# Loading seven of twelve strided row ends tensor by tensor, and keeping pieces of the channel mix out of the last six modes

## The chip, the cores and the metric

One core of a Trainium2 chip runs one program. The metric is the device time of one execution in microseconds (us). A profiled span is some 1.8 us shorter than the time of the same run, because it leaves out what lies before the first and after the last instruction. Spans are used for where time goes, times for how much. In the views, PE is the engine for matmuls (PEld its weight loads), DVE, ACT and POOL are the vector, scalar and GpSimd engines; `L547` is line 547 of the kernel.

## The reference

Local and strided causal attention (8 batches, 8 heads, 576 positions, head size 64) feeds a spectral layer: 64 complex 512 x 512 weight matrices, one for each mode, then an inverse transform and a channel mix.

```python
def _attn_ref(q, k, v):
    ...
    mask_local = (rel >= 0) & (rel < stride)                       # heads 0 to 3
    mask_strided = (rel >= 0) & (pos[None, :] % stride == pos[:, None] % stride)
    ...                                                            # softmax, times v

def _moe_ref(x, w_r, w_i, w_ch):
    X = np.fft.rfft(x, axis=1)
    Xr, Xi = np.real(X[:, :64]), np.imag(X[:, :64])
    Yr = einsum('bmd,mde->bme', Xr, w_r) - einsum('bmd,mde->bme', Xi, w_i)
    Yi = einsum('bmd,mde->bme', Xr, w_i) + einsum('bmd,mde->bme', Xi, w_r)
    Y[:, :64] = Yr + 1j * Yi
    u = x + np.fft.irfft(Y, n=S, axis=1)
    return u + np.maximum(u @ w_ch, 0.0)
```

## The kernel before

All large loads go out from GpSimd in one order. The strided heads of q, k and v come two batches at a time: a body of 64 partitions, and the **rest** of 8 partitions, each for two batches ("two tensors" below). The other q, k and v loads are the local heads, 128 partitions with rows of 1152 elements. The weights are tiles of two modes.

```python
def load_str(b, nb):
    for vi in (2, 0, 1):                         # v, q, k
        n = 3 * (b % 4) + SLOT[vi]
        two = ring[:, n : n + 4 : 3, :]          # two batches
        src = SRC[vi][b - b % 2 : b - b % 2 + 2, 4:8].rearrange(
            "b h (c r) d -> (h c) b (r d)", r=32)
        if nb == 2:
            nc.gpsimd.dma_start(two[0:64], src[0:64])
        else:
            nc.gpsimd.dma_start(ring[0:64, n, :], src[0:64, b % 2])
        if b % 2 == 0:
            nc.gpsimd.dma_start(two[64:72], src[64:72])      # the rest
```

With b = 0, 2, 4, 6 and three tensors there are twelve rests. In the second half of the kernel (the second 256 input channels), each mode is 16 small matmuls on its weight tile; between modes the PE does 76 pieces of other work (turns and pieces of the channel mix), and then the first matmuls of the tail.

```python
LATE = 10
first = len(work) - 2 * LATE
for m in range(NM - 3):                          # NM = 64
    mode(1, m)
    if m < NM - 3 - LATE:
        upto = -(-first * (m + 1) // (NM - 3 - LATE))
    else:
        upto = first + 2 * (m - (NM - 4 - LATE))
    for w in work[n:upto]:
        w()
    n = upto
    if m >= 16 and m % 16 in (4, 8):
        spec(m // 16 - 1, 0 if m % 16 == 4 else 1)   # inverse transform of 16 modes
# ...
for i in range(3):
    if i < 2:
        v_early(i)
    u_early(i)
warm = psum("v")
# ...
for m in range(NM - 3, NM):
    mode(1, m)
again(2)                                         # matmuls that only keep the clock up
spec_last(0)                                     # last 16 modes; then the tail
```

The softmax here doesn't subtract the row's maximum and nothing guards it: scores larger than these inputs give would overflow.

## Time and profile before

| | before |
|---|---|
| time, median of 4 runs | 436.77 us (436.56 to 436.91) |
| profiled span | 434.8 us |
| written by DMA | 92.16 MB |
| last weights land | 393.77 us |
| last-spectrum matmuls (`spec_last`) start | 398.02 us |
| from there to the end of the span | 36.8 us |

Read the table from the bottom: the end of the kernel has a fixed length, so what counts is when `spec_last` starts, and that needs the last weights and a free PE. The prediction below shows the page's slices and the chain of this kernel.

### The profile page before, as it was taken

The page shows a single profiled execution, that of the slowest core. Times are in us where ns is not written, and L with a number is a line of the kernel's source. Part 1 is how long each engine was busy: PE and PEld are TensorE (multiplying, and loading weights), DVE is VectorE, ACT ScalarE, POOL GpSimd, SP SyncE. Part 2 cuts the span into 40 slices and gives each one's busy share as a digit, 9 for nine tenths or more (in the row PEclk, how much of TensorE's full clock was granted, in tenths as well). Part 3 has the DMA queues.
Part 4 walks back from the last instruction along what each step waited for, and adds up shares of the span by engine and source line. Part 5 has one row for each costly group of instructions (what it writes and reads, how often), then busy time and mean ns, then how long its engine had stood idle before and what let it go on. Part 6 is the DMA issues. An engine that isn't in the chain of part 4 may idle for free.

```text
span 434.8 us, 12063 instructions
## 1 busy us (share of the span) xinstructions
PE 334.7 (77%) x5289; PEld 241.1 (55%) x5289; DVE 215.0 (49%) x466; ACT 188.0 (43%) x353; POOL 129.3 (30%) x208
## 2 busy tenths in 40 slices
PE   1987988789876879787865567679596769888994
PEld 1865776667765666665753345445454445554442
DVE  2788788744452242442511034244335443764895
ACT  1587678635542433534440302113313312443883
POOL 6423332323232222222222222222222222200893
PEclk9999899869895585988885559585769687999999
DMA  8999999999999999999999999999999999980787
GB/s 174 210 212 213 214 212 213 211 210 212 214 214 212 214 213 214 214 213 214 214 213 213 213 213 214 214 214 213 213 213 214 213 213 215 213 176 13 268 316 287
DMA packets 28995, 92.16 MB, mean 212 GB/s; under 512 B 4048, under 2 KB 5072, under 8 KB 28944
## 3 DMA queue, kind: packets, MB, share of 16 engines
q0 software_dynamic: 24704, 81.28, 94.2%
q1 hardware_dynamic: 3440, 9.46, 5.8%
q10 hardware_dynamic: 800, 0.67, 0.6%
q8 instruction: 41, 0.67, 0.6%
q14 instruction: 10, 0.08, 0.0%
HBM read 163.22 MB, written 9.44 MB: 397 GB/s over the span
## 4 chain that ended last, share of the span: by engine, by line
DMA 73%; PE 19%; DVE 2%; issue 2%; ACT 1%; POOL 1%; DVEq 0%; POOLq 0%
DMA wt<-in_moe_w_i_dram 51%; DMA ring<-in_v_dram 7%; DMA ring<-in_k_dram 6%; DMA wt<-in_moe_w_r_dram 4%; DMA ring<-in_q_dram 4%; PE sc L645 3%; PE y L547 3%; PE v L688 2%; PE u L688 2%; PE v L890 2%; PE y L514 1%; PE tp L653 1%; DVE yy L678 1%; PE u L911 1%; DVE xT L597 1%
## 5 line engine op out<-in xcount | busy, mean ns | idle before, releaser
L547 PE MATMUL y<-X,wt 128*128 128x16 f16 (+1 forms) x2048 | 82.4, 192 | 63.5 <-DMA wt<-in_moe_w_i_dram 60.9
L547 PEld LDWEIGHTS <-wt 128*128 128x128 f16 (+1 forms) x2048 | 72.6, 103 | 75.6 <-issue 72.3
L196 POOL DMA_DIRECT2D wt<-in_moe_w_r_dram x62 | 36.5, 589 | 142.2 <-PE y L547 63.1
L196 POOL DMA_DIRECT2D wt<-in_moe_w_i_dram x60 | 35.4, 590 | 70.6 <-DMA wt<-in_moe_w_i_dram 57.9
L654 ACT ACTIVATE v<-sc 128x512 f16<-128x512 f32 x32 | 18.9, 597 | 86.1 <-PE sc L645 86.0
L645 PE MATMUL sc<-w_cp,xT 128*128 128x512 f16 (+1 forms) x160 | 51.3, 450 | 0.4 <-DVE xT L617 0.4
L471 ACT ACTIVATE PL<-sc 128x480 f16<-128x480 f32 (+1 forms) x48 | 27.6, 579 | 47.4 <-PE sc L457 46.9
L655 DVE COPY xo<-tp 128x512 f16<-128x512 f16 x32 | 22.1, 692 | 45.5 <-PE tp L653 45.5
L250 DVE TENSOR_TENSOR xb<-av,rec 90x256 f16<-90x256 f32 (+2 forms) x80 | 36.0, 450 | 2.8
L249 DVE RECIPROCAL rec<-av 90x4 f32<-90x4 f32 (+2 forms) x80 | 14.7, 183 | 42.1 <-PE av L486 31.3
L402 DVE COPY qT<-tp 128x576 f16<-128x576 f16 x16 | 12.0, 758 | 42.8 <-PE tp L395 39.4
L260 ACT ACTIVATE v<-tp 128x640 f16<-128x640 f16 (+1 forms) x24 | 19.4, 808 | 21.2 <-PE tp L429 17.8
L395 PE MATMUL tp<-cI_s,ring 64*64 64x64 f16 x864 | 26.4, 210 | 2.2 <-issue 1.4
L360 ACT ACTIVATE PL<-sc 90x360 f16<-90x360 f32 (+1 forms) x48 | 22.7, 490 | 5.6 <-PE sc L353 4.9
L922 DVE TENSOR_TENSOR osb<-u,rl 128x512 f32<-128x512 f32 x36 | 23.6, 688 | 2.6 <-PE u L688 1.3
L395 PEld LDWEIGHTS <-ring 64*64 64x64 f16 x864 | 20.6, 122 | 7.4 <-issue 4.4
L905 POOL TENSOR_TENSOR rl<-rl,xo 128x512 f32<-128x512 f32 x16 | 18.3, 1156 | 20.5 <-ACT rl L903 20.2
L441 PE MATMUL sc<-cMl_s,cI_s 128*128 128x480 f16 (+1 forms) x48 | 22.4, 467 | 1.6 <-ACT X L260 1.6
L260 ACT ACTIVATE kz<-tp 64x360 f16<-64x360 f16 (+1 forms) x32 | 19.0, 595 | 10.2 <-PE tp L395 8.6
L457 PE MATMUL sc<-qT,kz 128*128 128x160 f16 (+1 forms) x160 | 22.6, 267 | 0.2 <-issue 0.2
L645 PEld LDWEIGHTS <-xT 128*128 128x128 f16 (+1 forms) x160 | 14.5, 109 | 14.6 <-issue 5.7
L285 PE MATMUL tp<-cI_s,ring 72*128 72x72 f16 x256 | 15.1, 206 | 9.5 <-DMA ring<-in_v_dram 8.0
(103 smaller groups left out, 647.8 us busy)
## 6 DMA issues: line engine op xcount, KB each, us to landing
wt<-in_moe_w_r_dram POOLq DMA_DIRECT2D x62, 512.0 KB, 18.9
wt<-in_moe_w_i_dram POOLq DMA_DIRECT2D x60, 512.0 KB, 19.4
out_dram<-osb SPq DMA_DIRECT2D x14, 512.0 KB, 2.7
ring<-in_v_dram POOLq DMA_DIRECT2D x8, 288.0 KB, 13.4
ring<-in_q_dram POOLq DMA_DIRECT2D x8, 288.0 KB, 13.6
ring<-in_k_dram POOLq DMA_DIRECT2D x8, 288.0 KB, 13.2
ring<-in_v_dram POOLq DMA_DIRECT2D x3, 512.0 KB, 15.5
ring<-in_q_dram POOLq DMA_DIRECT2D x3, 512.0 KB, 14.9
```

The costliest lines, as they stand in the source:

```text
L196: nc.gpsimd.dma_start(dst, rows)
L250: nc.vector.tensor_tensor(out=dst, in0=val.rearrange("p h (q c) -> p h c q", c=4), in1=rec[0:n, 0:pieces] .to_broadcast((n, pieces, 64)) . ...
L260: nc.scalar.activation(out=out, in_=in_, func=ACTF.Copy)
L360: nc.scalar.activation(out=PS[0:n, ds(POFF[t], 4 * n)], in_=scp[0:n, 0 : 4 * n], func=ACTF.Exp, scale=SCALE,)
L395: nc.tensor.transpose(tp[ds(64 * hp, 64), ds(64 * i, 64)], qn[ds(64 * hp, 64), ds(64 * (9 * g + i), 64)], idn[ds(64 * hp, 64), ds(64 * hp, ...
L441: nc.tensor.matmul(scp[:, 0 : n * times].rearrange("p (h x) -> p h x", h=times), idn, mask_rows("cMl", n, times), start=True, stop=False,)
L457: nc.tensor.matmul(scp[:, ds(col, n)], kzs[par][:, hp, ds(s0, 128)], qTs[par][:, ds(s0, n)], start=False, stop=(i == len(todo) - 1),)
L471: nc.scalar.activation(out=dst, in_=src, func=ACTF.Exp, scale=SCALE)
L547: nc.tensor.matmul(yv[:, mi, e, :], wt[pr, XC[c], ds(128 * e, 128)], Xh[half][pr, c, :, :, m], start=(c == 0), stop=(c == 3),)
L645: nc.tensor.matmul(vp[pr, :], xT[:, ch, cols], w_chs["cp"][:, ch, :], start=(ch == 0), stop=(ch == 3),)
L655: nc.vector.tensor_copy(out=xo[pr].rearrange("p (h q c) -> p h q c", h=2, c=4), in_=tp[pr, 0:512].rearrange("p (h c q) -> p h q c", h=2, c=4),
L922: nc.vector.tensor_tensor(out=osb[:, t % 2, :], in0=up, in1=rls[b, t][:, t % 2, :], op=AluOp.add)
```

## The change

Its intent: spread the small rests better over the DMA engines, and leave nothing but weights and PE work for them in the last six modes. The pieces must then be done three modes sooner; `LATE` goes from 10 to 12, and the first matmuls of the tail move in between the last modes, with a few more of the matmuls that keep the clock up.

```diff
--- before.py
+++ after.py
@@ -227,8 +227,14 @@
                 nc.gpsimd.dma_start(two[0:64], src[0:64])
             else:
                 nc.gpsimd.dma_start(ring[0:64, n, :], src[0:64, b % 2])
-            if b % 2 == 0:
+
+
+
+            if b % 2 == 0 and 3 * (b // 2) + SLOT[vi] < 5:
                 nc.gpsimd.dma_start(two[64:72], src[64:72])
+            elif b % 2 == 0:
+                for j in range(2):
+                    nc.gpsimd.dma_start(two[64:72, j], src[64:72, j])
 
     def load_loc(*bs):
         for b in bs:
@@ -836,14 +842,15 @@
 
     n = 0
 
-    LATE = 10
+    LATE = 12
+    END = NM - 6
     first = len(work) - 2 * LATE
-    for m in range(NM - 3):
+    for m in range(END):
         mode(1, m)
-        if m < NM - 3 - LATE:
-            upto = -(-first * (m + 1) // (NM - 3 - LATE))
+        if m < END - LATE:
+            upto = -(-first * (m + 1) // (END - LATE))
         else:
-            upto = first + 2 * (m - (NM - 4 - LATE))
+            upto = first + 2 * (m + 1 - (END - LATE))
         for w in work[n:upto]:
             w()
         n = upto
@@ -940,20 +947,22 @@
                 osb,
             )
 
-    for i in range(3):
-        if i < 2:
-            v_early(i)
-        u_early(i)
-    warm = psum("v")
 
 
     def again(n):
         for i in range(n):
             nc.tensor.matmul(warm, idn, v0s[0][:, 2, :], start=True, stop=True)
 
-    for m in range(NM - 3, NM):
+    early = [lambda i=i: v_early(i) for i in range(2)]
+    early += [lambda i=i: u_early(i) for i in range(3)]
+    warm = psum("v")
+    for m in range(END, NM):
         mode(1, m)
-    again(2)
+        if m < END + 2:
+            for w in early[3 * (m - END) : 3 * (m - END) + 3]:
+                w()
+        else:
+            again(3 if m < NM - 1 else 2)
     spec_last(0)
     again(3)
     v_early(2, warm)
```

Line numbers shift with it: `spec_last`'s matmuls are L882 before and L889 after, a mode is L547 and L553.

## The prediction

> **What bounds the kernel now.** I read three views in this order: the slices, the chain of the end in order of time, and the GpSimd timeline beside it. The slices first (PEclk is the granted TensorE clock in tenths, a slice is 434.8 / 40 = 10.87 us):
>
> ```profile
> PEclk9999899869895585988885559585769687999999
> DMA  8999999999999999999999999999999999980787
> GB/s 174 210 212 213 214 212 213 211 210 212 214 214 212 214 213 214 214 213 214 214 213 213 213 213 214 214 214 213 213 213 214 213 213 215 213 176 13 268 316 287
> ```
>
> For 35 slices the DMA engines are full at 213 GB/s written (the loads convert f32 to f16, so twice that is read). These are the weights, and no rearrangement of compute changes that part. The time is then set by two things: when the last weight lands, and how long after it the kernel ends. The last loads, in the GpSimd timeline (start us, us, engine, line, operation, in brackets the idle time before and its releaser):
>
> ```profile
> 381.48 0.52 POOL L199 DMA_DIRECT2D wt<-in_moe_w_i_dram  x1 [1.94 <-DMA wt<-in_moe_w_r_dram]
> 384.00 0.52 POOL L199 DMA_DIRECT2D wt<-in_moe_w_i_dram  x1 [2.00 <-DMA wt<-in_moe_w_i_dram]
> DMA to landing us min/median/max: 9.8/10.7/11.7
> ```
>
> (The last line is the answer for the weight tile in the window from 380.) Issued at 384.00 and 9.8 us under way, the last weights land at 393.8. The chain then shows (start us, us, what):
>
> ```profile
> 390.47 0.48 PE y L547 x16
> 390.95 0.86 PE sc L645 x4
> ...
> 393.28 0.70 DVE xoh L655
> 394.03 0.39 PE v L890
> ...
> 394.85 0.43 PE u L911 x2
> 395.28 0.49 PE y L547 x16
> 395.86 0.57 DVE YT L575
> 396.47 1.12 PE y L547 x32
> 397.59 0.43 PE v L952 x2
> 398.02 0.99 PE y L882 x4
> ```
>
> Each L547 group of 16 is one mode. Mode 60 runs at 390.47, then come its two pieces of the channel mix (L645 and L653), the DVE copy that frees their PSUM banks, the five early matmuls, mode 61 at 395.28, and modes 62 and 63 only from 396.47. Nothing in this stretch waits for a DMA: all weights are there from 393.8, and mode 63 starts at about 397.0. So in the last 10 us the **PE queue is the bound**, not the weight stream. From the last-spectrum matmuls (L882, 398.02) to the end at 434.8 are 36.8 us that the change does not touch.
>
> **Why the last weights come as late as 393.8.** The trace keeps sixteen completion records for each load, one for each DMA engine. For the last load eight are between 387.37 and 389.36 and the other eight between 392.82 and 393.77: half of the engines run 5.1 us behind (means of the two halves). This gap is 0.7 us at 14 us, about 0.95 at 60 us, 2.0 at 140, 3.5 at 229, 4.2 at 301 and 5.1 at the end, so it grows steadily long after the rests are loaded. What grows with it are the 41 packets of the instruction queue, 16 KB and about 0.94 us each: their times repeat in a pattern of eight, and 34 fall between 60 and 390 us, so 34 x 0.94 / 8 = 4.0 us on each of eight engines. That is the growth. Following the packets by their spacing (305 ns from one 4 KB packet to the next on an engine), the engines that carry instruction packets are those that get the data of the even rests (v of batch pair 4, k of 4, q of 6); I trust this grouping only fairly.
>
> **What the Trainium skill says.** (1) "DMA: Bandwidth & Descriptors", section "Why a DMA increments its semaphore by 16 and not by 1": the number of engines is the largest k up to 16 that divides the slowest dimensions, so eight partitions give k = 8, on consecutive engines from a round-robin cursor; but some direct copies from GpSimd get k = 16 with partitions/16 rounded up per engine, which for eight partitions would be always the first eight engines. The trace agrees with the first for the rests of two tensors: between 37 and 64 us an engine shows two packets for one rest and none for the next, in turn. For a rest of one tensor no instruction of this kernel tells which of the two holds. (2) "TensorE: Matmul & The Clock Gate", Part 1: the clock is either full or half, decided over windows of 3.4 us of activity. The trace agrees: the clock records are 1.0 or 0.5 and change in multiples of 3.41 us; half from 354.4 to 364.7, then full until 432.9. (3) Same page, "Back-to-back issue gap": 216 ns for 512 columns warm; here four take 0.86 us, 215 ns each.
>
> **Part 1, the rests.** Seven of twelve loads of 8 partitions x 2 tensors (16 packets) become two of 8 packets each. No byte is added; 7 more GpSimd issues of 0.52 to 0.58 us lie in a queue that spends most of its time waiting for older loads. Eight loads are in flight at most (each issue waits for the one eight before), so the small ones cut the depth from some 12 to some 8 us of data around 25 to 55 us; the waits there are at most 2.6 us, so no starvation. What is left is the distribution. Now the late seven put 3 x 2 = 6 packets on the slow half and 8 on the fast half.
> - If single loads go always to the fast eight: 0 and 14. The slow half ends 6 x 0.305 = 1.8 us earlier (393.8 to 391.9), the fast half 1.8 later (389.4 to 391.2). Nearly balanced: this would explain why it is just seven.
> - If the cursor alternates: 7 and 7, the slow half 0.3 us later.
> - If always to the slow eight: 14 and 0, 2.4 us later, 396.2.
> I give them 0.55, 0.35 and 0.10; the odd count "seven of twelve" is what speaks for the first.
>
> **Part 2, the last six modes.** 76 pieces exist. Before, 56 go over modes 0 to 50 and two to each of 51 to 60; after, 52 over modes 0 to 45 and two to each of 46 to 57. So six pieces (about 5 us of full-clock PE work at 0.86 + 0.22 for a mix piece, 0.5 to 0.6 for a turn) move from modes 58 to 60 to modes 46 to 50. There is room there: between 350 and 360 PE is busy 5.17 of 10 us and waits twice 2.4 us for weights. But part of that room is at half clock (354.4 to 361.2 at least, mix piece 2.1 us instead of 1.08).
>
> My schedule by hand: mode 46 at 354.4 as now; modes 46 and 47 with pieces at half clock until some 361.5; then 0.48 + 2 pieces each at full clock plus two spectra (about 1.5 us with their waits): pieces end at about 387.0, instead of 393.2. Then mode 58, the DVE copy (0.7), three early matmuls, mode 59, two early, mode 60 at 389.6, three warming matmuls (0.65), mode 61 at 390.7, its DVE add (0.57) to 391.9, mode 62 at 392, three more warming ones, PE ready for mode 63 at 393.1. After mode 63 come 0.64 for a mode that has waited (0.49 if not) and two warming ones (0.43): L882 starts 0.95 to 1.2 us after mode 63 does.
>
> - Fast-eight case: weights at 391.9, PE at 393.1: L882 at 394.0, a gain of 4.0 us (4.9 if my PE estimate is 1 us too slow).
> - Alternating: weights at 394.1, L882 at 395.3: gain 2.7; with weights where they are, 3.0.
> - Slow-eight: weights at 396.2, L882 at 397.4: gain 0.6.
> Weighted: 0.55 x 4.1 + 0.35 x 2.8 + 0.10 x 0.6 = 3.3 us, and 436.75 - 3.3 = 433.4.
>
> **The rivals.** (a) *The PE stays the bound.* If the half clock lasts longer than 361, each further 3.4 us window costs some 1.7 us of PE work, pieces end near 389 and mode 63 comes 1 to 2 us later: total 434 to 435. For it: the clock record of before stays half until 364.7. Against: PE would be fuller there, and full windows ended the half clock. (b) *The clock falls at the end.* With the pieces gone PE may sit idle for weights in the last modes; a half clock over the tail's first window would add 1 to 2 us after 394. The added warming matmuls (3 x 0.215 = 0.65 us after a mode) are there against it. For it: a window with busy share 0.29 at 351 to 354 was followed by half clock. Total about 434.5. (c) *Hidden anyway:* the weight stream ends where it does and modes 58 to 63 can only wait for it: then only the 3 us between 393.8 and 397.0 are to be had, 433.7. (d) *Late fetches:* the loads for modes 60 and 61 go out when mode 51 frees its buffer; mode 51 comes some 4 us later (370.5 instead of 366), but at 366 the loads in flight last to 383, so nothing starves.
>
> **Range and chances.** Bottom: fast-eight case with no PE bound, 436.75 - 5.3 = 431.4. Top: slow-eight, or one rival added to a small gain, 435.8. 2% are 8.7 us. The gain is capped near 6 us by the weight stream (even a perfectly balanced one ends at (388.4 + 393.4) / 2, about 391), and a loss of 8.7 has no mechanism. So: faster 0.02, same 0.97, slower 0.01.
>
> **What would show it.** Right: no L645 between the last six modes; L882 at 394 to 395.5; the span after it still 36.8 us. The sixteen completions of the last load tell the three cases of part 1 apart: gap about 1.4 us (fast eight), about 5.7 (alternating), near 10 (slow eight). Clock full from about 361 to 433. Wrong: mode 63 waiting for pieces or for the DVE add instead of for weights, half clock in 387 to 400, or a DMA slice under 205 GB/s between 20 and 380 us.

## More of the kernel before

One more view is needed for what follows, the busy time by stretch. Its columns: start and end in us, length, busy us and instructions of five engines, granted TensorE clock, busy share of the DMA engines (over 1, since packets of one engine overlap), GB/s written.

```profile
core 0: us, PE busy (x) PEld busy (x) DVE busy (x) ACT busy (x) POOL busy (x), PEclk, DMA share, GB/s
54.00:98.00 44.00, 35.63 (x671) 29.16 (x670) 31.76 (x83) 28.55 (x61) 13.92 (x25) 0.88 1.08 211
98.00:131.00 33.00, 28.16 (x672) 22.90 (x670) 15.40 (x30) 17.15 (x31) 10.44 (x18) 0.95 1.09 213
131.00:142.00 11.00, 7.45 (x157) 6.26 (x158) 2.80 (x6) 3.22 (x6) 2.71 (x5) 0.57 1.06 213
142.00:380.00 238.00, 179.13 (x2857) 126.87 (x2854) 89.54 (x183) 75.73 (x135) 56.46 (x97) 0.73 1.06 213
```

The stretch from 54 to 98 us is the one in which the strided and local tensors of q, k and v are loaded between weights. Here it looks like every other: 211 GB/s.

## The result, and the profile after

The changed kernel took **439.79 us** (439.7 to 440.37, 4 runs) against 436.77 us for the kernel before in the same rounds. The ratio is 1.0072 (95% interval 1.0055 to 1.0090). All ratios here are the mean time of one kernel's runs over the mean of the other's runs of the same rounds, so not quite the ratio of the medians quoted. The prediction was 433.4 us with a range of 431.4 to 435.8: outside the range, and of the wrong sign. All outputs are right.

First the slices of the changed kernel's page, which answer to those in the prediction:

```profile
PEclk9999899869786588788875558698978868989999
DMA  8999999999999999999999999999999999991687
GB/s 175 207 211 213 211 198 197 197 190 211 209 212 203 214 213 215 213 214 213 214 211 210 214 214 214 214 214 213 213 214 213 214 213 214 214 196 29 264 314 285
```

Slices 6 to 9 (54 to 98 us) are down from 210 to 214 to between 190 and 198 GB/s, while the digit of the DMA share stays 9. Here are the same stretches of the changed kernel, in the columns explained above:

```profile
54.00:98.00 44.00, 34.54 (x628) 28.37 (x629) 30.91 (x81) 28.59 (x61) 14.49 (x26) 0.89 1.10 196
98.00:131.00 33.00, 28.81 (x668) 23.57 (x665) 13.71 (x28) 16.11 (x30) 10.63 (x19) 0.86 1.09 211
131.00:142.00 11.00, 5.89 (x134) 4.79 (x132) 3.56 (x7) 3.01 (x6) 2.96 (x6) 0.66 1.09 204
142.00:380.00 238.00, 176.76 (x2897) 125.86 (x2894) 91.04 (x185) 75.31 (x136) 56.18 (x97) 0.76 1.07 213
```

From 54 to 98 us the DMA engines are *busier* (1.10 against 1.08) and write *less* (196 against 211 GB/s). On the whole they do not run dry: their packets take longer. In this stretch the mean 4 KB packet took 351 ns against 324 before, and the mean 2304-byte packet 215 ns against 192, while the medians are the same 324 and 192 in both. So packets are slow in bursts, and in a burst those of all engines are (all 44 that started between 74 and 75 us). The bursts sit where the stream changes from weights (4 KB packets) to local loads (2304-byte packets) or back: at 69 to 71, 73 to 75, 79 to 82, 88 to 90, 93 to 96, 112 to 114 and 131 to 133 us. Cut into steps of 1 us, the stretch from 54 to 142 us has 447 slow packets (4 KB over 400 ns, 2304 bytes over 240) of 2137 in the steps with both sizes, and 113 of 3503 in the others; the kernel before makes the same changes with 9 slow of 1165.

For about 1 us engines did run dry, which the average hides. The first line is the changed kernel, the second the kernel before:

```profile
60.50:61.50 1.00, 0.63 (x13) 0.38 (x10) 0.93 (x4) 1.00 (x3) 0.74 (x2) 1.00 0.90 156
60.50:61.50 1.00, 0.34 (x5) 0.30 (x6) 0.96 (x3) 0.91 (x3) 0.26 (x1) 1.00 1.02 205
```

The share fell to 0.90, and with (213 - 156) / 213 of 1 us it cost some 0.3 us. Counting bytes, the DMA queue of the changed kernel is 0.3 us behind that of before at 58 us, 3.7 us at 100 us, 4.5 us at 139 us, and from there to the end between 4.5 and 4.8 us behind.

What came before the bursts is in the completion records, sixteen for a load. I sort the sixteen times of a load and call the mean of the later eight less the mean of the earlier eight its **gap**:

| rest landing at about | before | after |
|---|---|---|
| 21 us (last one of two tensors in both) | 0.65 | 0.40 |
| 24 us (the first one cut) | 0.69 | 0.46 |
| 40 us | 0.86 | 1.06 |
| 46 us | 0.84 | 1.67 |
| 59 us | 1.04 | 2.53 |
| 65 us | 0.96 | 3.74 |

With rests of two tensors the gap stays near 1 us. With rests of one tensor it grows, by (3.74 - 0.40) / 14 = 0.24 us for each on average, though until 54 us packets have almost their normal length (the mean 4 KB packet from 40 to 54 us took 326 ns, 324 before). The ends of the sixteen times tell more. From 38 us on, each single rest moves the first of them by 0.17 to 0.19 us and the last by 0.24 to 0.33; the rests of two tensors before moved the first by 0.17 to 0.18 and by 0.64 to 0.68 us in turn. So I read it that single rests go to the same eight engines every time; the experiments below put that to the test.

Then the end. The last weight load goes out later, in the GpSimd timeline of the changed kernel (start us, us, engine, line, operation, idle time before it and its releaser):

```profile
384.55 0.52 POOL L199 DMA_DIRECT2D wt<-in_moe_w_r_dram  x1 [1.68 <-DMA wt<-in_moe_w_i_dram]
387.01 0.52 POOL L199 DMA_DIRECT2D wt<-in_moe_w_i_dram  x1 [1.94 <-DMA wt<-in_moe_w_r_dram]
389.47 0.52 POOL L199 DMA_DIRECT2D wt<-in_moe_w_i_dram  x1 [1.94 <-DMA wt<-in_moe_w_i_dram]
```

It was issued at 389.47 us where it was 384.00, and landed at 399.10 us where it was 393.77: 5.3 us later. This is the chain of waits of the changed kernel in order of time (start us, us, what):

```profile
390.46 0.88 PE av L673 x4
...
391.37 0.58 ACT zz L266
...
394.39 0.60 ACT v0h L660
...
395.04 0.59 PE v L897 x2
...
400.31 0.47 PE y L553 x16
400.78 0.43 PE v L954 x2
401.21 0.99 PE y L889 x4
```

Mode 63 runs at 400.31 and the last-spectrum matmuls at 401.21 us, 2.11 us after the last weights; before, it was 398.02 - 393.77 = 4.25 us. The tail is 438.1 - 401.21 = 36.9 us (36.8 before). So the account closes: weights +5.33, wait after them -2.14, tail +0.1, together +3.3, and the spans differ by 438.1 - 434.8 = 3.3 us.

### The profile page after: what moved, and what is told of

Read it like the earlier page. It is cut to its first block, busy times and chain, and to the rows that moved or that the text cites. A ratio compares the mean times of both kernels' runs of the same rounds, so it can differ in the third digit from the quotient of the medians.

```text
span 438.1 us, 12090 instructions
## 1 busy us (share of the span) xinstructions
PE 335.0 (76%) x5298; PEld 241.3 (55%) x5298; DVE 215.3 (49%) x466; ACT 188.1 (43%) x353; POOL 132.5 (30%) x215
## 4 chain that ended last, share of the span: by engine, by line
DMA 69%; PE 19%; DVE 5%; ACT 2%; issue 2%; POOL 1%; DVEq 0%; POOLq 0%
DMA wt<-in_moe_w_i_dram 49%; DMA wt<-in_moe_w_r_dram 10%; DMA ring<-in_k_dram 4%; DMA ring<-in_v_dram 3%; PE sc L651 3%; DMA ring<-in_q_dram 3%; PE y L553 3%; PE u L694 2%; PE v L694 2%; PE v L897 2%; DVE xb L256 1%; DVE kz L298 1%; PE tp L401 1%; PE tp L659 1%; ACT X L266 1%
## 5 line engine op out<-in xcount | busy, mean ns | idle before, releaser
L553 PE MATMUL y<-X,wt 128*128 128x16 f16 (+1 forms) x2048 | 82.3, 192 | 66.4 <-DMA wt<-in_moe_w_i_dram 65.2
L553 PEld LDWEIGHTS <-wt 128*128 128x128 f16 (+1 forms) x2048 | 72.4, 103 | 78.8 <-issue 56.2
L660 ACT ACTIVATE v<-sc 128x512 f16<-128x512 f32 x32 | 19.1, 597 | 81.8 <-PE sc L651 81.7
L266 ACT ACTIVATE v<-tp 128x640 f16<-128x640 f16 (+1 forms) x24 | 19.4, 807 | 21.8 <-PE tp L435 18.6
L603 DVE COPY xT<-tp 128x512 f16<-128x512 f16 x16 | 11.0, 689 | 28.1 <-PE tp L597 15.0
L266 ACT ACTIVATE kz<-tp 64x360 f16<-64x360 f16 (+1 forms) x32 | 19.0, 593 | 11.5 <-PE tp L401 10.1
```

The lines of the kernel that those rows point to most:

```text
L266: nc.scalar.activation(out=out, in_=in_, func=ACTF.Copy)
L553: nc.tensor.matmul(yv[:, mi, e, :], wt[pr, XC[c], ds(128 * e, 128)], Xh[half][pr, c, :, :, m], start=(c == 0), stop=(c == 3),)
```

## The experiments

Each kernel ran beside the kernel before on the same chip. **Theory A**: the single rests all land on the same eight engines; the engines drift apart, and while q, k and v loads are under way this makes packets slow on all of them. **Rivals**: the window of eight loads in flight holds too few bytes with small loads in it, so engines run dry; more loads cost by themselves; part 2 or the shifted loads at the end do it. (In the expectations of e1 and e3, theory A still says that the other eight engines run dry; slow packets take that place from e5 on.)

| run | median us | ratio to before (95%) | largest gap, 54 to 100 us | GB/s, 54 to 98 us | mean 4 KB packet there, ns |
|---|---|---|---|---|---|
| before | 436.8 to 437.6 | | 1.14 | 211 | 324 |
| the change | 439.79 | 1.0072 (1.0055 to 1.0090) | 3.74 | 196 | 351 |
| e1, part 1 alone | 442.08 | 1.0115 (1.0096 to 1.0134) | 3.34 | 196 | 352 |
| e3, single rests spaced | 445.52 | 1.0192 (1.0170 to 1.0214) | 5.29 | 190 | 352 |
| e10, three single pairs | 439.58 | 1.0023 (0.9998 to 1.0048) | 2.38 | 204 | 342 |
| e6, foreign small loads early | 439.35 | 1.0048 (1.0027 to 1.0069) | 2.09 | 208 | 331 |
| e5, rests cut by columns | 437.36 | 1.0015 (0.9993 to 1.0038) | 1.03 | 211 | 325 |
| e9, the change with e5's cut | 434.70 | 0.9925 (0.9906 to 0.9945) | 1.17 | 211 | 324 |
| e4, seven tiny loads | 437.40 | 1.0013 (0.9994 to 1.0033) | 1.36 | 211 | 324 |
| e2, part 2 alone | 434.93 | 0.9953 (0.9932 to 0.9975) | 1.33 | 212 | 325 |
| e8, part 2 with LATE = 6 | 434.07 | 0.9925 (0.9909 to 0.9942) | 1.43 | 212 | 324 |
| e11, part 2 with LATE = 0 | 435.41 | 0.9945 (0.9926 to 0.9965) | 1.55 | 212 | 324 |

(One more, e7, tests late small loads and is told below.) The rows with a gap of up to 1.55 us have normal packets; those over 2 have slow ones, roughly the more the larger the gap.

### e1 and e2: the two parts alone

e1 is the kernel before with the first hunk of the diff alone, e2 with the other hunks alone.

> Part 1 alone (seven rests one by one, last modes as before). Theory A (the single rests shorten the load window and all land on the same eight engines, so the other eight run dry around 61 to 100 us): the last weights land some 5 us later than 393.8 and the time is 4 to 5.5 us over the kernel before, 441 to 442. Rival B (part 1 costs nothing much, part 2 is what slows the kernel): within 1 us of 436.8. Rival C (the two parts interact): anything else, such as no loss in the early 213 GB/s slices.

> Part 2 alone (rests in pairs as before). Theory A: weights land at 393.8 as before, L882's counterpart starts about 2.1 us after them instead of 4.25, so 434.3 to 434.8, 2 to 2.5 us faster than before. My recorded prediction would have it 3 us faster, 433.7. Rival B: slower than before by 1 us or more.

The page of e1 (GB/s by slice), then that of e2:

```profile
GB/s 171 203 209 211 211 199 196 193 196 211 208 212 207 216 212 214 213 213 214 214 210 213 213 214 215 214 212 213 214 214 214 213 214 213 213 179 9 264 311 285
```

```profile
GB/s 175 209 212 212 214 213 212 211 210 212 215 210 214 213 214 214 213 214 213 213 213 213 214 213 215 214 213 213 213 214 213 213 214 213 213 171 14 266 315 287
```

Part 1 alone brings the dip and costs 1.15%; part 2 alone has no dip and gains 0.47%. Together they make 1.0115 x 0.9953 = 1.0067, and 1.0072 was measured: the parts add up, and the loss is part 1's. In e1 the last weights landed at 400.50 us.

### e3: the single rests spaced out

The single rests of part 1 are put in a list and issued one at a time, each behind a large load, so that two seldom stand side by side in the window of loads in flight (the last two do, issued at 61.15 and 63.52 us).

```diff
+    def rest():
+        if rests:
+            nc.gpsimd.dma_start(*rests.pop(0))
...
             elif b % 2 == 0:
                 for j in range(2):
-                    nc.gpsimd.dma_start(two[64:72, j], src[64:72, j])
+                    rests.append((two[64:72, j], src[64:72, j]))
+            rest()          # and after each weight load, and before the local loads of a batch
```

> As e1, but the single rests are issued one at a time, each after a large load, so that a window of eight loads holds at least four large ones. Same number of loads, same data on the same engines. Theory A (running dry needs the short window): the dip below 205 GB/s at 60 to 100 us is gone, the gap between the two halves of the engines grows by the rests' 3 to 4 us and stays; total within 2.5 us of before, the loss being only the later slow half. Rival D (the uneven engines alone cost the bandwidth): same loss as e1.

```profile
GB/s 175 204 212 212 212 204 173 199 182 211 204 207 207 213 213 215 214 213 213 214 205 212 215 213 214 213 213 214 215 213 213 213 213 215 215 147 3 258 310 284
```

It got worse: 1.0192, a slice at 173 GB/s, loads whose sixteen completions lie up to 7.2 us apart, and mean 2304-byte packets of 235 ns. A window of in-flight loads that is too short would have been eased by this, and the loss grew. That rival is therefore not the main cause; e4 and e5 test it with the window as short as in e1.

### e4 and e5: more loads, the same placement

e4 adds seven small loads (64 partitions x 16 elements, into scratch) where the second single rests would be. e5 issues each of the seven rests as two loads too, but cut by columns, so that each still has 8 partitions x 2 tensors:

```diff
+                for j in range(2):
+                    half = ds(1024 * j, 1024)
+                    nc.gpsimd.dma_start(two[64:72, :, half], src[64:72, :, half])
```

> The kernel before (rests in pairs, last modes as before) plus seven loads of 64 rows of 64 bytes where part 1 adds a load: the window is shortened in the same way but no data is placed unevenly. Theory A (both are needed): less than 1.5 us over before, no dip or a small one. Rival E (the number of loads in the window alone): 3 us or more over before with the dip at 60 to 100 us.

> The kernel before, with the same seven rests split into two loads each, but by halves of the columns instead of by tensor: each load keeps its 8 x 2 rows, so it should keep the placement of the pairs (one eight of the engines, then the other). As many loads as part 1 and the same bytes. Theory A' (it is the always-same eight engines that hurt, not the count of loads): within 1.2 us of before, no dip of GB/s at 60 to 100 us, spread of the landings about 2 us there. Rival E' (more and smaller rest loads hurt however they are placed): 3 to 5 us slower as in e1.

```profile
GB/s 173 204 212 212 212 213 211 211 211 212 214 213 212 215 213 215 212 214 213 214 213 212 214 214 213 213 215 212 214 213 213 215 213 215 212 180 15 267 320 283
```

Neither has a dip, and both intervals hold 1. e5 has exactly the loads of e1 in number, order and bytes; only the shape differs, and with it the engines that they go to. Its completions lie 1.4 to 2.5 us apart, its gap does not grow. Number and size of the loads and the depth of the window are therefore not the cause; what is left is the placement that the shape brings, as the gap shows it. One thing more differs: e5's rests are packets of 2 KB, those of e1 of 4 KB. The uncut rests of before are packets of 4 KB too, and do no harm.

### e6 and e7: unevenness without touching the rests

e6 leaves the rests as before and adds seven loads of 8 rows of other data in front of the places where q, k and v are read; e7 adds fourteen such loads (8 rows of 1152) in the second half, where only weights are loaded.

```diff
+                    nc.gpsimd.dma_start(ring[72:80, n, :],
+                        moe_w_r[m, 0:32, :].rearrange("(p c) e -> p (c e)", c=4))      # e6
...
+            if 84 <= i < 112:
+                nc.gpsimd.dma_start(<8 dead rows>, <8 rows of 1152 from moe_w_r>)      # e7
```

> The kernel before with its paired rests, plus seven loads of 8 rows of 2048 (of weights, into ring rows that nothing reads) where part 1 adds a load: the unevenness of single loads without touching the rests. 7 x 0.305 = 2.1 us more on one eight of the engines, half of what part 1 puts there, and 0.23 MB more in all (1.1 us at 213 GB/s). Theory A': slow packets and a dip at 60 to 100 us appear, less than in e1; 2 to 4 us slower. Rival F (the rests themselves, being late or awaited, cost the time): at most 1.3 us slower, no dip.

> The kernel before plus fourteen loads of 8 rows of 1152 between weight loads of the second half (about 230 to 310 us), where no loads of q, k and v are in flight. 14 x 0.173 = 2.4 us more on whatever engines take them. If single loads always land on the same eight: the spread between the engines changes by some 2 us over that stretch. If slow packets come from the spread alone they appear there too and GB/s dips; if they need loads of q, k, v in flight (row size 2304 written) beside weights, GB/s stays at 213. Time: 0 to 2.5 us slower by where the eight lie against the engines that end last.

The page of e6, then that of e7:

```profile
GB/s 177 209 213 213 212 211 212 207 202 212 213 212 213 214 213 215 212 214 213 215 210 212 214 213 214 214 213 214 213 214 213 214 214 213 213 184 16 267 316 285
```

```profile
GB/s 177 206 211 213 214 212 213 211 210 213 214 212 214 213 214 214 213 214 213 214 212 213 213 214 213 214 213 213 213 212 212 212 214 213 214 161 19 250 335 263
```

e6 brings a small dip (202 GB/s in slice 9) and slow bursts at 78, 88 and 92 us, with the rests as they were. It cost 0.48%, 2.1 us, of which its own 0.23 MB at 213 GB/s explain 1.1; the rest is hardly clear of noise in time (the interval begins at 0.27%), but in the trace the queue falls 0.9 us behind over and above these bytes. e7 (439.67 us, ratio 1.0063, 1.0043 to 1.0082) has no burst although its completions come up to 7.4 us apart (7 of 3244 4 KB packets between 286 and 350 us took over 450 ns); its 2.7 us are its own bytes (0.26 MB, 1.2 us) and later last landings. So engines that are apart are not enough: from 54 us on the bursts came where the stream changed between weights and large loads of another row size. These were nearly always q, k and v, but not only: at the end of the one load of channel-mix weights (1 KB packets) 15 of 47 packets of 4 KB took over 400 ns between 230 and 231 us in the changed kernel, and 32 of 33 between 232 and 233 us in e3 (none of the kernel before from 230 to 233 us). e7 also shows a smaller thing. Its gap went from 4.1 down to 3.2 us and not up, while the spread went from 5.6 to 6.9 us: the eight engines of small single loads are not the eight that carry the packets of the instruction queue, but overlap with them in part. That reading is inferred, since the records do not name the engine.

### e9: the whole change with the rests cut by columns

The changed kernel with e5's three lines in place of its two.

> The changed kernel, both parts, with its seven single rests cut by columns (8 partitions x 2 tensors x half a row) instead of by tensor: same number of loads, same bytes of each, only the placement differs. Theory A (the single rests all land on the same eight DMA engines, and the unevenness makes the packets slow): no dip in GB/s at 54 to 142 us, and the time of part 2 alone (434.9) plus the 0.3 us of run e5, 434.5 to 436, some 4.5 us less than the changed kernel. Rival (the extra loads cost by themselves once part 2 is there too, or the two parts hurt each other): 438 or more.

```profile
GB/s 172 206 212 212 213 211 212 211 211 212 214 211 214 214 213 214 215 213 213 215 211 213 214 213 214 214 214 214 213 213 214 214 213 213 215 194 35 267 322 283
```

The dip is gone, the last weights land at 393.96 us, and the change becomes a gain: 434.70 us, ratio 0.9925. Against 1.0072 for the change as it was, the shape of the rests alone is worth 1.5%, some 6 us (4.9 us between the two profiled spans, 5.1 us between the last landings). This settles where the loss comes from: same loads, same bytes, same order, another shape.

### e10: three single pairs in place of seven

Part 1 with `< 9` in place of `< 5`, so that only the last three rests are cut by tensor.

> Part 1 alone, but only the last three of the twelve pairs are loaded one by one, so the gap of the halves should grow by 6 x 0.23 = 1.4 us instead of 3.3. If the slow packets need a gap of some 3 us (a threshold): no dip, and 436.5 to 437.5. If the loss goes in proportion to the single loads: 6/14 of 5.0 us, 439.1. If the number of q and k loads still to come while the engines are apart counts, less than in proportion.

```profile
GB/s 173 206 212 213 213 210 201 201 203 212 214 207 213 214 213 213 215 214 213 214 212 212 214 213 213 215 214 212 213 213 214 213 214 213 213 169 5 265 312 287
```

The gap grew from 0.80 to 1.72 us over the six single loads, and there was a dip to 201 to 203 GB/s in slices 7 to 9: the queue fell 2.3 us behind. A threshold at 3 us is refuted; in the stream the loss follows the dose (6/14 of e1's 5.0 us are 2.1). In time this run is not clear: its runs lie between 437.56 and 440.06 us, the profiled one was one of the two slowest (its clock was half from 398.9 to 402.3 us, in the tail), and the interval holds 1.

### e8 and e11: how many pieces late

Part 2 alone with another `LATE`: 6 in e8 and 0 in e11, where the change has 12.

> Part 2 alone with its pieces spread more evenly: two pieces a mode only over the six modes before the last six (LATE 6 instead of 12), so more pieces are done before. In e2 the PE still ended its pieces 1 to 3 us too late for the last weights. If that is what is left, 1 to 3 us faster than e2, 432 to 434. Rival: with fewer pieces late the PE idles, the clock is half more often in the last modes, and the time is e2's or worse.

> Part 2 alone with no thicker end: 76 pieces spread evenly over modes 0 to 57 (LATE = 0; the change has 12, run e8 had 6 and took 434.07). If the pieces' end before mode 58 is what counts, fewer of them late helps further: 433.3 to 434.1, with last-spectrum matmuls 1.2 us after the last weights. If the last weights are the bound from LATE = 6 on: the same as e8, 434.0 to 434.3. If the clock falls in the idle last modes, or early pieces hold the modes and so the weights up: 435 or more.

The PE timeline of e8 at the last modes (start us, us, engine, line, operation, out<-in, idle before and releaser):

```profile
388.58 0.59 PE L894 MATMUL v<-v,cI_s 128*128 128x512 f16 x2 [0.37 <-ACT v0h L657]
...
393.18 0.64 PE L550 MATMUL y<-X,wt 128*128 128x16 f16 x16 [0.64 <-DMA wt<-in_moe_w_i_dram]
393.65 0.81 PE L951 MATMUL v<-v,cI_s 128*128 128x512 f16 x3
394.47 0.64 PE L550 MATMUL y<-X,wt 128*128 128x16 f16 x16
...
395.50 1.04 PE L886 MATMUL y<-w_ch,YT 128*128 128x512 f16 x4
```

and that of e11:

```profile
386.91 0.59 PE L894 MATMUL v<-v,cI_s 128*128 128x512 f16 x2 [0.88 <-ACT v0h L657]
...
393.78 0.64 PE L550 MATMUL y<-X,wt 128*128 128x16 f16 x16 [2.38 <-DMA wt<-in_moe_w_i_dram]
394.26 1.44 PE L951 MATMUL v<-v,cI_s 128*128 128x512 f16 x3
395.50 0.68 PE L550 MATMUL y<-X,wt 128*128 128x16 f16 x16
396.02 1.01 PE L951 MATMUL v<-v,cI_s 128*128 128x512 f16 x2
396.83 0.43 PE L886 MATMUL y<-w_ch,YT 128*128 128x512 f16 x1
```

In e8 mode 62 waits 0.64 us for weights and mode 63 follows them at once (landed 394.34, run 394.47): weights and PE are ready within 0.13 us of each other, and `spec_last` starts 1.16 us after the weights. This version beats both kernels, at 434.07 us. In e11 the pieces end 1.7 us sooner still (386.91 for the first tail matmul), the PE idles 2.38 us, and the clock drops: three warming matmuls take 1.44 us where they took 0.81, and `spec_last` starts 1.89 us after weights that landed at 394.94. The clock record of e11 is half from 393.5 to 396.9 us, one window of 3.4 us. In the window before the fall (390.1 to 393.5) the PE was busy for some 1.3 us.

## Why the prediction was wrong, point by point

**The bound before, and the tail: right.** With the weights landing as before (393.70 us in e2), moving PE work alone gained 0.47%, so the PE queue did hold the end; and the tail kept its length (36.8, 36.9 us).

**"What is left is the distribution": wrong, and the step that failed.** Part 1 was taken to move a few packets between two halves of engines, with the total rate unchanged. But with the engines apart, packets became slow on all of them from 54 to 142 us (196 in place of 211 GB/s up to 98 us), and the queue lost 4.2 of its 4.7 us there. "So no starvation" failed too, though it cost little: engines ran dry from 60.5 to 61.5 us, for some 0.3 us. The text named the sign itself ("a DMA slice under 205 GB/s between 20 and 380 us") but gave it no chance.

**Where single rests go: the most likely case was half right.** The fixed eight engines that got 0.55 did come true in the sense that the cursor does not alternate: the exception in the Trainium skill, "DMA: Bandwidth & Descriptors", section "Why a DMA increments its semaphore by 16 and not by 1", fits (gap +0.24 us for each of fourteen). But those eight are not "the fast eight": the gap grew from the first and was 3.3 us for the last load, where the three cases had 1.4, 5.7 and 10. The first and last completion of a load came further apart and not closer: 7.8 to 8.0 us for the weights landing between 362 and 397 us, against 6.2 to 6.5 before (those landing between 362 and 392 us; for the very last load alone it is 6.1 against 6.4). The grouping that I trusted "only fairly" was wrong, and "seven of twelve" is no sign of a balance.

**Part 2: the mechanism was right, one term was 2 us too small.** With weights where they are the estimate was a gain of 3.0 us; measured were 0.47% (2.1 us) in e2, and 1.0015 - 0.9925 = 0.9% (3.9 us) between e5 and e9, in different rounds. The cleanest check of the steps is e9, whose last weights landed at 393.96 us, where the alternating case had 394.1. Its PE timeline:

```profile
381.87 1.87 PE L652 MATMUL sc<-w_cp,xT 128*128 128x512 f16 x4
...
387.84 1.05 PE L652 MATMUL sc<-w_cp,xT 128*64 128x512 f16 x4
388.73 0.39 PE L660 MATMUL tp<-cI_s,xT 128*64 128x128 f16 x4
389.05 0.65 PE L554 MATMUL y<-X,wt 128*128 128x16 f16 x16
390.06 0.59 PE L898 MATMUL v<-v,cI_s 128*128 128x512 f16 x2 [0.37 <-ACT v0h L661]
...
391.57 0.59 PE L554 MATMUL y<-X,wt 128*128 128x16 f16 x16
...
395.12 0.64 PE L554 MATMUL y<-X,wt 128*128 128x16 f16 x16
...
396.14 1.04 PE L890 MATMUL y<-w_ch,YT 128*128 128x512 f16 x4
```

Pieces were to end at 387.0 and mode 63 to come at 393.1, 6.1 us later. They ended at 389.05 (start of the next mode, L554) and mode 63 came at 395.12, 6.07 us later: the schedule by hand held to the tenth, and the term that failed is the end of the pieces, by 2.05 us. `spec_last` was to start at 395.3 and started at 396.14, bound by the PE and not by the weights. The changed kernel shows the same with the late stream on top: 389.05 + 4.7 = 393.8, and its pieces ended at 394.03.

A word on the chain of the changed kernel above. From 391.37 to 394.99 us it goes through ACT (four copies of the spectrum of mode 56, L266, then the last piece's own two, L660), and I first took these 3.6 us for the cost. But the PE worked on the last two pieces meanwhile and waited for ACT only 0.36 us; in e9, in the fence above, it is the 0.37 us before 390.06. A chain that runs through an engine says that it ended last, not by how much.

**Rival (a), half clock for longer: a half window is most of it, but a later one.** The prediction had the clock full from about 361 us and put 1.7 us on each further window of 3.4 us at half. The records have half from 380.7 to 384.1 us in e9 (four matmuls of a piece in 1.87 us at 381.87, 1.05 at 387.84), from 368.9 to 372.3 and 382.5 to 385.9 in the profiled run of e2, the slowest of its six, and from 385.5 to 388.9 in the changed kernel; before had none from 364.7 us to the tail, e8 none from 371.3. In e9's window the PE was busy for all 3.4 us, so by this estimate it makes 1.7 of the 2.05 us; no run takes it out alone. What set such a window in one kernel and not in another is not shown. In e9, the changed kernel and the second one of e2, the 3.4 us before held 2.3 to 2.4 us of PE work, with a wait of 0.8 us for a DVE copy; but before e2's first they held 3.1.

**Rival (b)**, a falling clock from too few pieces, came among the runs with part 2 only with LATE = 0 (e11). **Rival (d)**, late fetches starving the stream, did not show: outside 54 to 142 us the rates are equal.

**The sum.** Predicted -3.3 us (its weighted sum takes 4.1 and 2.8 us for two cases that it had worked out as 4.0 and 2.7, which is 0.1 us); measured +3.0. The stream was to give between +2.4 and -1.9 us and gave +5.3; the PE side was to give back up to 3.0 and gave 2.1.

**What stays open.** Why packets of *all* engines are slow when engines are apart and the stream changes from one kind of load to another. Engines that work on different loads at once could collide in reading their sources, but no view here shows the source side, so this is only a guess. Also open is how much of the loss e10's dose makes in time.

## What to carry to other kernels

When a load of few partitions is cut, keep the shape by which it spreads over the DMA engines: with the same bytes and the same count, 8 partitions x 2 rows alternated between the engines and 8 x 1 did not, and that was worth 1.5%. When bytes per second fall while the busy share stays, compare the mean with the median length of a packet, and the first with the last completion of a load, before blaming depth, and look whether the slow packets sit where the stream changes from one kind of load to another. Work taken out of the last stretch has to be fitted in somewhere else, and what it costs there depends on the clock of that stretch; with too little left, the clock falls in the last one.

## What the Trainium skill lacked or had wrong

- "DMA: Bandwidth & Descriptors" speaks of "some direct copies" and does not say which: here loads of 8 partitions x 1 row kept to the same eight engines (gap from 0.40 to 3.74 us over fourteen of them), loads of 8 x 2 did not (gap near 1 us throughout).
- No page that I read has the slowing of all engines after uneven placement: 4 KB packets of 351 instead of 324 ns on average, 196 instead of 211 GB/s, with medians unchanged.
- No page that I read says what the instruction queue takes from the loads: 41 packets of 16 KB and about 0.94 us each in a run, their times in a pattern of eight. By my reading they, with what the rests add, set the last weights' completions 6.4 us apart before any change.
- "TensorE: Matmul & The Clock Gate" gives an idle window of about 3.4 us for the fall to half clock; in e11 the 3.4 us before the fall held some 1.3 us of PE work, in e9 2.4 and in e2 once 3.1.
